# Attention values with v stationary: softmax weights stream, row sums from added weights, x turned back by a matmul

## The chip, the cores and the metric

The kernel runs on one core of a Trainium2 chip. The metric is device time in microseconds (us) from the first to the last instruction. The core has five engines with queues of their own: TensorE (PE in the profile; PEld is its weight load), VectorE (DVE), ScalarE (ACT), GpSimd (POOL) and SyncE (SP, which here only issues transfers). A TensorE matmul `mm(out, lhsT, rhs)` holds `lhsT` stationary and streams `rhs` through: the columns of `lhsT` become the partitions of the output, and `rhs` is what moves. All data are f32, and each f32 matmul appears as two records in the trace.

## The reference, cut to what matters

Attention over 8 batches, 8 heads, 576 positions and a head size of 64, with a bias from cumulated sums; then a mixture of 8 experts in which each token goes to one expert, either its own best (by the logits) or that of the token before it.

```python
scores = q @ k.T / sqrt(64)                        # causal, plus bias -(cum[i] - cum[j])
attn = exp(scores - max) / (sum + 1e-9)
x = (attn @ v) as (B, S, H*D)                      # D = 512 per token
logits = x @ w_gate;  local = sigmoid(x @ w_local)
for b, s in order:                                 # the expert is carried along the sequence
    e = argmax(logits[b, s]) if s == 0 or local < 0.5 else expert of s - 1
    out[b, s] = softmax(logits)[e] * (relu(x @ w1[e]) @ w2[e])
```

## The kernel before

Two heads make a pair, and there are 32 pairs (4 of each batch). Scores are computed turned: keys on partitions, queries along the columns, so that `sc` (the exponentials, called weights below) has keys on partitions. For one pair they come in four units of two PSUM banks each. `scores(n, u)` multiplies both heads (64 rows of the array each), ScalarE takes the exponentials, GpSimd zeroes the half above the diagonal. The last 64 keys against the last 64 queries are a tile of their own, `sct`.

```python
UNITS = (((1, 0, P, 2 * P), (0, 0, 0, 2 * P)),          # (key chunk, group, first query, end)
         ((0, 1, 2 * P, S), (3, 1, 3 * P, S)),
         ((1, 1, 2 * P, S),), ((2, 1, 2 * P, S),))
VW = DH + E + 2                                         # 64 of v, 9 value logits, a one: 74

def values(n, t):                                       # t: a tile of 128 queries; the fifth has 64
    if t < NF:
        for h in range(2):
            for c in range(t + 1):
                mm(po[:, t % 2, h, :], lhsT=weights(n, c, t, h), rhs=va[:, c, 2 * hp + h, :], ...)   # L369
        if t % 2:
            nc.vector.reciprocal(rec, po[:, :, :, VW - 1])
            for to, a, z in (("x", 0, DH), ("l", DH, VW - 1)):
                nc.vector.tensor_tensor(xs[b, to][...], po[:, :, :, a:z], rec..., op=Alu.mult)      # L375
    else:
        for c in range(NF):
            for h in range(2):
                mm(po[h * TL : h * TL + TL, :], lhsT=weights(n, c, NF, h), rhs=va[:, c, 2 * hp + h, :], ...)  # L381
        for h in range(2):
            mm(po[d, :], lhsT=scs[n, "t"][d, :], rhs=vl[d, hp, :], ...)                             # L385
        # ... cut: reciprocal and two products
```

Here the weights are stationary (128 columns) and v moves (74 columns). So that no product with `w_gate` is needed later, v carries its own logits: `value_logits` multiplies v (turned, `vT`, its own load) by `w_gate` and `w_local` (L284) and turns the result back into `va` (L296), once per batch. The one in the last column gives the sum of the weights. `logits` adds up the heads, and for the 64-row tile `logits_tail` folds two halves by a matmul (L407, `ltp`).

```python
for n in range(NPAIR + 1):                              # one attention step
    # ... cut: loads of the next batch
    scores(n, 0); scores(n, 1)
    values(n - 1, 0..2)
    # ... logits_tail once per batch; plan: sorting stages, scatters, weight loads
    scores(n, 2); scores(n, 3)
    values(n - 1, 3..4)
    # ... value_logits (hp >= 2), store and logits at a batch's end; plan
```

The tokens are sorted by expert while attention still runs: groups of batches (0, 1) and (2, 3, 4) pass through stages (choose, rows, hold, rank, gates) and scatter their rows of x to a buffer in memory; batches 5 to 7 are sorted in hooks of the expert stage. Four experts' first blocks of 128 tokens ("early" blocks) are fetched before attention ends.

```python
for bs, n0 in (((0, 1), 9), ((2, 3, 4), 21)):           # ... stages and two scatters per half step
at(28, 1, sort.early)
at(20, 0, lambda bank: load_weights(nc, ready["w"][0], w1, w2, 0))
last = sort.group((5, 6, 7), xs)
experts(..., [("early", e) for e in range(4)] + [("further", i) for i in range(SURE)], hooks, ...)

# experts: a block of 128 tokens
turn_x(i):   four transposes of x into PSUM, copied to xT            # L1023, L1025
layer1(i):   64 records hp <- w (stationary), xT (128 columns)       # L1040
layer2(i):   16 records yp <- hT (stationary), w (512 columns)       # L1052
load(i + 2): 4.2 MB of one expert's weights in 8 transfers           # L960
```

Of the kernel before, what the change touches and what calls it, by code (L numbers as in the profile page):

```python
# [32 lines left out]
XW = D + 2  # L33
R = N + P
EARLY = 4
SURE = NBLK - 2 - EARLY
MASKED = -1e9
VW = DH + E + 2
WR = 16
# [3 lines left out]

UNITS = (
    ((1, 0, P, 2 * P), (0, 0, 0, 2 * P)),
# [3 lines left out]
)  # L49


@with_exitstack
def kernel(
# [6 lines left out]
    vT: bass.AP,  # L60
# [19 lines left out]
    recs = const.tile([P, NPAIR, 2 * NF + 1], F32, name="recs")  # L80
# [3 lines left out]
    with ExitStack() as main:  # L84
# [4 lines left out]
        def new_x(b):  # L89
            xs[b] = keep.tile([P, NF, XW], F32, name="xb"), keep.tile([TL, XW], F32, name="xt")  # L90
            return xs[b]
# [7 lines left out]
        for bs, n0 in (((0, 1), 9), ((2, 3, 4), 21)):  # L99
            g = sort.group(bs, xs)  # L100
            for f, i in zip(g.stages, (1, 2, 3, 4, 4)):
                at(n0 + i // 2, i % 2, f)
            for i, f in enumerate(g.scatters):
                i = 5 + i // 2
                at(n0 + i // 2, i % 2, f)
        at(3, 1, sort.constants)
        at(28, 1, sort.early)
        gx = main.enter_context(tc.tile_pool(name="gx", bufs=5))
        ready = {"w": {0: wf.tile([P, DK * F + FK * D], F32, name="w")}, "x": {}}
        at(20, 0, lambda bank: load_weights(nc, ready["w"][0], w1, w2, 0))  # L110

        def fetch_early(bank):
            for e in range(EARLY):
                ready["x"][e] = gx.tile([P, XW], F32, name="xg")
                nc.sync.dma_start(ready["x"][e], rows_d[e * R : e * R + P, :])

        at(30, 0, fetch_early)
        last = sort.group((5, 6, 7), xs)

        tail = attention(tc, q, k, vm, vt, vT, s, w_gate, w_local, ident, lg, recs, const, new_x, plan)  # L120
# [5 lines left out]
                [("early", e) for e in range(EARLY)] + [("further", i) for i in range(SURE)], hooks, wf, gx, ready)  # L126
# [6 lines left out]
    wrong = nc.values_load(out_of[0:1, 0:1], min_val=0, max_val=P * NPAIR * (2 * NF + 1),  # L133
                           skip_runtime_bounds_check_because="a count of elements")
    with tc.If(wrong > 0):
        attention_general(tc, q, k, vm, vt, s, w_gate, w_local, cum_d, x_d, ident, lg)
        with ExitStack() as again:
# [8 lines left out]
            for bs in (range(0, 4), range(4, 8)):  # L146
                xs = {b: (pool.tile([P, NF, XW], F32, name=f"xb{b % 4}"), pool.tile([TL, XW], F32, name=f"xt{b % 4}"))
                      for b in bs}
                for b in bs:
                    r0 = b * S  # L150
                    nc.sync.dma_start(xs[b][0][:, :, :D], x_d[r0 : r0 + TS, :].rearrange("(t p) d -> p t d", p=P))
                    nc.sync.dma_start(xs[b][1][:, :D], x_d[r0 + TS : r0 + S, :])
                g = sort.group(bs, xs)
                for f in (*g.stages, *g.scatters):
                    f(bank)
# [6 lines left out]
def attention(ctx, tc, q, k, vm, vt, vT, s, w_gate, w_local, ident, lg, recs, keep, new_x, plan):  # L162
# [20 lines left out]
    p_vT = pool("p_vT", 1)  # L183
# [3 lines left out]
    ps_s = pool("ps_s", 3, space=PSUM)  # L187
    ps_o = pool("ps_o", 2, space=PSUM)

    ins, vTs, scs, vws, xs = {}, {}, {}, {}, {}  # L190

    first, rest, whole = slice(0, 1), slice(1, HP), slice(0, HP)

    def new_batch(b):
        qk = p_in.tile([P, 2, HP, S], F32, name="qk")
        ins[b] = [qk[:, i] for i in range(2)]
        vTs[b] = p_vT.tile([P, HP, S], F32, name="vTb")
# [5 lines left out]
    def load_vT(b, p):  # L203
        nc.sync.dma_start(vTs[b][:, p], vT[b][:, p])

    def load_v(b, p, eng=nc.sync):
        h = slice(2 * p.start, 2 * p.stop)
        for c in (slice(0, NF),) if p == whole else (slice(c, c + 1) for c in range(NF)):
            eng.dma_start(vas[b % 2][:, c, h, :DH], vm[b][:, c, h])

    def load_vl(b, eng=nc.sync):
        eng.dma_start(vls[b % 2][:, :, :DH], vt[b])
# [5 lines left out]
    vas = [(once if i else p_va).tile([P, NF, H, VW], F32, name=f"va{i}") for i in range(2)]  # L218
    vls = [once.tile([P, HP, VW], F32, name=f"vl{i}") for i in range(2)]
# [7 lines left out]
    load_v(0, first, nc.scalar)  # L227
    load_vT(0, first)
    load_vl(0, nc.scalar)
    load_qk(0, slice(1, 2), nc.scalar)  # L230
    load_vT(0, rest)
    load_v(0, rest)
    for i in range(2, HP):
        load_qk(0, slice(i, i + 1))
    wbd = once.tile([P, HP, 2 * WR], F32, name="wbd")
    nc.gpsimd.memset(wbd, 0.0)
    for h in range(2):
        for w, a, z in ((w_gate, 0, E), (w_local, E, E + 1)):
            nc.gpsimd.dma_start(wbd[h * DH : h * DH + DH, :, h * WR + a : h * WR + z],
                                w.rearrange("(a h d) e -> h d a e", h=2, d=DH)[h])  # L240
    for t in (*vas, *vls):
        nc.gpsimd.memset(t[..., VW - 1 : VW], 1.0)

    idle = ps_s.tile([P, 2, 512], F32, name="idle", tag="s")
    for i in range(10):
        mm(idle[:, 0, :P], lhsT=ident, rhs=ident, start=True, stop=True)
    fold = keep.tile([P, TL], F32, name="fold")
    nc.vector.tensor_tensor(fold, ident[:, :TL], ident[:, TL:], op=Alu.add)
# [3 lines left out]

# [4 lines left out]
    for g, (q0, q1) in enumerate(GROUPS):  # L257
        rel = t_in.tile([BH, q1], F32, name=f"rel{g}")
        nc.vector.tensor_scalar(rel, cum[:, :q1], cum[:, MIDS[g] : MIDS[g] + 1], None, Alu.subtract)
        for c in range(min(NF, q1 // P)):  # L260
            tr(bps[:, at : at + BH], rel[:, c * P : (c + 1) * P], ident[:BH, :BH])
            bias_of[g, c] = at
            at += BH
    for h in range(2):
        mm(bps[h * TL : h * TL + TL, at : at + NPAIR], lhsT=rel[:, TS:],
           rhs=ident[:BH, :BH].rearrange("k (n h) -> k h n", h=2)[:, h], start=True, stop=True)
    bias_of["tail"] = at
    bias = once.tile([P, at + NPAIR], F32, name="bias")
    nc.vector.tensor_copy(bias, bps[:, : at + NPAIR])
    tmp.close()  # L270
    p_sc = pool("p_sc", 2, reuse_waits="tile")
    p_sm = pool("p_sm", 2)

    def value_logits(b, step, p=whole):

        if b >= B:
            return
        va, vl = vas[b % 2], vls[b % 2]
        rows = slice(32 * p.start, 32 * p.stop)
        if step == 0:  # L280
            ps = ps_s.tile([P, 2, 512], F32, name="vwp", tag="s").rearrange("p a c -> p (a c)")
            for a, z in ((0, 512), (512, S)):
                for hp in range(p.start, p.stop):
                    mm(ps[hp * 32 : hp * 32 + 32, a:z], lhsT=wbd[:, hp, :], rhs=vTs[b][:, hp, a:z],  # L284
                       start=True, stop=True)
            if p.start == 0:
                vws[b] = p_sm.tile([P, NB * P], F32, name="vw")
            for i in range(p.start, p.stop) if p.start else (0,):
                r = slice(32 * i, 32 * i + 32) if p.start else rows
                nc.vector.tensor_copy(vws[b][r, :S], ps[r, :S])  # L290
                nc.vector.tensor_copy(vws[b][r, S:], ps[r, TS:S])
            return
        pt = ps_s.tile([P, 2, 512], F32, name="vwt", tag="s").rearrange("p a c -> p (a c)")
        n = rows.stop
        for c in range(NB):
            tr(pt[:, c * P : c * P + n], vws[b][:n, c * P : (c + 1) * P], ident[:n, :n])  # L296
        keyed = pt[:, : NB * P].rearrange("p (c h e) -> p c h e", c=NB, e=WR)
        hs = slice(2 * p.start, 2 * p.stop)
        nc.vector.tensor_copy(va[:, :, hs, DH : DH + E + 1], keyed[:, :NF, hs, : E + 1])
        for h in range(2):  # L300
            d = slice(h * TL, h * TL + TL)
            nc.vector.tensor_copy(vl[d, p, DH : DH + E + 1],
                                  keyed[d, NF, :, : E + 1].rearrange("p (a h) e -> p a h e", h=2)[:, p, h])

    def scores(n, u):
# [3 lines left out]
        heads = [slice(DH * h, DH * h + DH) for h in range(2)]  # L309
        tail = u == 0  # L310
        ps = ps_s.tile([P, 2, 512], F32, name="ps", tag="s")
        w = sum(q1 - q0 for _, _, q0, q1 in UNITS[u])
        sc = scs[n, u] = p_sc.tile([P, 2, w], F32, name=f"sc{u}")
        at, places = 0, []
        for c, g, q0, q1 in UNITS[u]:
            for h, d in enumerate(heads):
                mm(ps[:, h, at : at + q1 - q0], lhsT=kb[d, hp, c * P : c * P + P], rhs=qb[d, hp, q0:q1],  # L317
                   start=True, stop=True)
            places.append((c, g, q0, at, at + q1 - q0))
            at += q1 - q0  # L320
        if tail:
            for d in heads:
                mm(ps[d, 0, at : at + TL], lhsT=kb[d, hp, TS:], rhs=qb[d, hp, TS:], start=True, stop=True)  # L323
        diag = []
        for c, g, q0, a, z in places:
            for h in range(2):
                i = bias_of[g, c] + 2 * n + h
                nc.scalar.activation(sc[:, h, a:z], ps[:, h, a:z], Act.Exp, bias=bias[:, i : i + 1], scale=scale)  # L328
# [786 lines left out]
```

## Time and profile before

Median of three runs: 962.62 us (961.43 to 965.38). The profiled execution spans 964.8 us.

| stage | from, to (us) | what runs |
|---|---|---|
| start | 0 to 8.5 | loads, bias from the cumulated sums |
| attention | 8.5 to 344 | 33 steps |
| experts | 344 to 965 | 41 blocks of 128 tokens |

How to read the lines in the following part. A group's line gives the source line, the engine, the operation, output<-inputs, the shapes (for a matmul: stationary rows*columns, then output) and how often it ran. A timeline line gives the start, the length, the instruction group merged over neighbours, and how many. "PE x <- y" in the list of waits is what TensorE waited for: total us, times, the longest. "issue" is a wait for nothing that the profile shows. "PEclk" is the share of full clock that TensorE was granted. Matmuls are pipelined, so the time between two starts says more than the length of one.

### The profile page before, as it was taken

The numbers are of one execution on the slowest core, as the hardware profiler recorded it, in microseconds if no ns is written. First come the engines' busy times: TensorE is split into PE (matmuls) and PEld (weight loads), VectorE is DVE, ScalarE is ACT, GpSimd is POOL, SyncE is SP. The second block draws the span as 40 slices with busy tenths as digits, with TensorE's granted clock in tenths as the row PEclk, the third lists the DMA queues.
The fourth block names the chain that finished last, engine by engine and source line by source line (L and its number), as shares of the span: only waits on it lengthen the run. The fifth ranks groups of instructions, "written<-read, shape, count | busy, mean of one in ns | idle before, by whom it ended". The sixth has DMA issues, their size and how long they took to land.

```text
span 964.8 us, 16728 instructions
## 1 busy us (share of the span) xinstructions
PE 927.7 (96%) x6538; PEld 698.9 (72%) x6538; DVE 209.8 (22%) x649; ACT 182.0 (19%) x465; POOL 171.9 (18%) x329
## 2 busy tenths in 40 slices
PE   8999998999979996999999999999999999999995
PEld 5787786877758884677777777777777777677672
DVE  3222432224313243121111111111111111111110
ACT  3454544444525400000000000000000000000000
POOL 2221143121352206011011011011011011011000
PEclk8999998999979998999999999999999999999998
DMA  9463262637541658988988988988988988988950
GB/s 272 130 213 148 55 222 80 203 151 226 186 138 44 232 202 293 314 305 326 351 303 323 352 296 324 344 309 317 340 320 324 344 311 317 344 308 322 352 209 20
DMA packets 78332, 245.30 MB, mean 254 GB/s; under 512 B 21245, under 2 KB 21277, under 8 KB 75552
## 3 DMA queue, kind: packets, MB, share of 16 engines
q1 hardware_dynamic: 66480, 214.30, 63.7%
q0 software_dynamic: 9312, 28.68, 8.0%
q10 hardware_dynamic: 2448, 1.11, 0.5%
q8 instruction: 56, 0.92, 0.4%
q14 instruction: 36, 0.29, 0.1%
HBM read 220.67 MB, written 23.64 MB: 253 GB/s over the span
## 4 chain that ended last, share of the span: by engine, by line
PE 79%; DMA 2%; issue 2%; POOL 1%; DVE 1%; POOLq 0%; DVEq 0%
PE hp L1040 31%; PE yp L1052 29%; PE po L369 8%; PE ps L317 5%; DMA x_rows<-xb,r_slot_i 2%; PE xp L1023 2%; PE pot L381 1%; PE pot L385 0%; PE vwp L284 0%; PE ps L323 0%; POOL x_rows L947 0%; PE bank L876 0%; POOL sc L334 0%; PE vwt L296 0%; PE ltp L407 0%
## 5 line engine op out<-in xcount | busy, mean ns | idle before, releaser
L1040 PEld LDWEIGHTS hp<-xT,w 128*128 128x128 f32 x2624 | 301.1, 192 | 30.9 <-issue 29.1
L1040 PE MATMUL hp<-xT,w 128*128 128x128 f32 x2624 | 304.1, 276 | 10.2 <-issue 8.7
L1052 PE MATMUL yp<-w,hT 128*128 128x512 f32 x656 | 295.5, 594 | 0.0
L1052 PEld LDWEIGHTS yp<-w,hT 128*128 128x128 f32 x656 | 119.0, 191 | 119.6 <-issue 119.4
L328 ACT ACTIVATE sc<-ps,bias 128x320 f32<-128x320 f32 (+3 forms) x384 | 151.3, 486 | 168.3 <-PE ps L323 88.1
L369 PEld LDWEIGHTS po<-va,sc 128*128 128x128 f32 x1280 | 149.8, 194 | 25.5 <-issue 20.9
L369 PE MATMUL po<-va,sc 128*128 128x74 f32 x1280 | 159.3, 280 | 3.8 <-POOL sc L334 3.8
L1045 ACT ACTIVATE hT<-hp 128x512 f32<-128x512 f32 x41 | 24.5, 597 | 560.3 <-PE hp L1040 532.2
L1058 POOL DMA_INDIRECT out_dram<-y,at x41 | 40.9, 997 | 497.0 <-DVE y L1057 483.9
L317 PE MATMUL ps<-qk 64*128 64x320 f32 (+3 forms) x768 | 113.9, 417 | 0.0
L1043 DVE TENSOR_SCALAR hT<-hp 128x512 f32<-128x512 f32 x41 | 28.3, 691 | 261.0 <-PE hp L1040 261.0
L334 POOL TENSOR_SCALAR_AFFINE_SELECT sc<-sc 128x256 f32<-128x256 f32 (+1 forms) x96 | 47.6, 496 | 198.7 <-ACT sc L328 197.1
L317 PEld LDWEIGHTS ps<-qk 64*128 64x128 f32 x768 | 63.2, 193 | 18.2 <-issue 2.9
L1057 DVE TENSOR_SCALAR y<-yp,xg 128x512 f32<-128x512 f32 x41 | 30.8, 750 | 114.5 <-PE yp L1052 114.3
L1025 DVE COPY xT<-xp 128x512 f32<-128x512 f32 x41 | 28.3, 691 | 119.7 <-PE xp L1023 119.6
L373 DVE RECIPROCAL recs<-po 128x4 f32<-128x4 f32 x64 | 11.7, 183 | 185.9 <-PE po L369 183.5
L1023 PEld LDWEIGHTS xp<-ident,xg 128*128 128x128 f32 x164 | 20.4, 141 | 20.6 <-issue 20.6
L947 POOL DMA_INDIRECT x_rows<-xb,r_slot_i x32 | 31.4, 981 | 8.4 <-issue 7.3
L375 DVE TENSOR_TENSOR xb<-po,recs 128x256 f32<-128x256 f32 x64 | 27.2, 425 | 11.0 <-DMA x_rows<-xb,r_slot_i 8.6
L1023 PE MATMUL xp<-ident,xg 128*128 128x128 f32 x164 | 24.7, 273 | 0.0
L1016 POOL DMA_DIRECT2D xg<-x_rows x37 | 22.1, 598 | 12.2 <-DMA w<-in_w_dram 9.8
L381 PE MATMUL pot<-va,sc 128*64 128x74 f32 x512 | 23.5, 234 | 0.0
(140 smaller groups left out, 255.4 us busy)
## 6 DMA issues: line engine op xcount, KB each, us to landing
w<-in_w_dram SPq DMA_DIRECT2D x328, 512.0 KB
xg<-x_rows POOLq DMA_DIRECT2D x37, 257.0 KB
qk<-in_q_dram SPq DMA_DIRECT2D x7, 1152.0 KB
qk<-in_k_dram SPq DMA_DIRECT2D x7, 1152.0 KB
vTb<-in_vT_dram SPq DMA_DIRECT2D x7, 1152.0 KB
va<-in_vm_dram SPq DMA_DIRECT2D x7, 1024.0 KB
x_rows<-r_empty SPq DMA_DIRECT2D x13, 257.0 KB
qk<-in_q_dram SPq DMA_DIRECT2D x4, 288.0 KB
```

Source lines behind the costliest of these rows:

```text
L317: mm(ps[:, h, at : at + q1 - q0], lhsT=kb[d, hp, c * P : c * P + P], rhs=qb[d, hp, q0:q1], start=True, stop=True)
L328: nc.scalar.activation(sc[:, h, a:z], ps[:, h, a:z], Act.Exp, bias=bias[:, i : i + 1], scale=scale)
L334: nc.gpsimd.affine_select(out=x, in_=x, compare_op=Alu.is_ge, fill=0.0, base=0, pattern=[[0, 2], [0, len(diag)], [1, P]], channel_multipli ...
L369: mm(po[:, t % 2, h, :], lhsT=weights(n, c, t, h), rhs=va[:, c, 2 * hp + h, :], start=(c == 0), stop=(c == t))
L381: mm(po[h * TL : h * TL + TL, :], lhsT=weights(n, c, NF, h), rhs=va[:, c, 2 * hp + h, :], start=(c == 0), stop=False)
L947: self.s.nc.gpsimd.indirect_dma_start(out=next(self.s.views)[:, :], out_offset=bass.IndirectOffsetOnAxis(ap=self.slot[:z, m : m + 1], axis=0),
L1023: tr(ps[:, c, :], xg[i][:, c * P : (c + 1) * P], ident)
L1025: nc.vector.tensor_copy(xT[i], ps)
L1040: mm(ps[:, j, :], lhsT=w[:, c, f], rhs=xT[i][:, c, :], start=(c == 0), stop=(c == DK - 1))
L1052: mm(ps, lhsT=h[:, c, :], rhs=w[:, c, :], start=(c == 0), stop=(c == FK - 1))
L1057: nc.vector.tensor_scalar_mul(y, ps, xg[i][:, D + 1 : D + 2])
L1058: nc.gpsimd.indirect_dma_start(out=outs[i][:, :], out_offset=bass.IndirectOffsetOnAxis(ap=at[i][:, 0:1], axis=0), in_=y[:, :], element_off ...
```

## The change

v becomes stationary and the weights move. A group of queries (0 to 255, or 256 to 575) is one PSUM bank with the two heads on partitions 0 to 63 and 64 to 127, so x comes out turned: head size on partitions, queries along columns. The tail tile is gone; instead the last 128 keys (`KEYS[NF] = S - P`, those already counted masked out by a bias of -1e9) meet the last 64 queries. v's logits, `vT` and their matmuls are gone too. The sums of the weights come from VectorE adding the chunks of keys, and then matmuls with a column of ones. x, still turned and not divided, is turned back by a matmul against `turn`, which holds an identity with `w_gate` and `w_local` beside it, so that x and its logits come out together; the product with the reciprocal follows. x's row has 8 pieces of 73 (64 and 9), 586 words with identity and gate, in place of 514.

```diff
-VW = DH + E + 2
+HW = DH + E + 1
+X0 = E + 1
+XI = H * HW
+XW = XI + 2
-EARLY = 4
+EARLY = (0, 0, 1, 1)
 UNITS = (
-    ((1, 0, P, 2 * P), (0, 0, 0, 2 * P)),
+    ((1, 0, P, 2 * P), (0, 0, 0, 2 * P), (NF, 1, TS, S)),
...
-        for bs, n0 in (((0, 1), 9), ((2, 3, 4), 21)):
+        for bs in ((0, 1), (2, 3), (4,), (5,)):
+            n0 = HP * bs[-1] + HP + 1
             g = sort.group(bs, xs)
-            for f, i in zip(g.stages, (1, 2, 3, 4, 4)):
+            for f, i in zip(g.stages, (1, 3, 5, 7, 8)):
...
-        at(20, 0, lambda bank: load_weights(nc, ready["w"][0], w1, w2, 0))
+        for i in range(8):
+            at(16 + i // 2, i % 2, lambda bank, i=i: load_weights(nc, w, w1, w2, EARLY[0], (i,)))
-        last = sort.group((5, 6, 7), xs)
+        last = sort.group((6, 7), xs)
...
-    ps_s = pool("ps_s", 3, space=PSUM)
-    ps_o = pool("ps_o", 2, space=PSUM)
+    ps_s = pool("ps_s", 2, space=PSUM)
+    ps_o = pool("ps_o", 1, space=PSUM)        # four tags: o0, o1, b0, b1
...
-    for i in range(10):
-        mm(idle[:, 0, :P], lhsT=ident, rhs=ident, start=True, stop=True)
+    spin(18)                                  # warm-up matmuls; 8 more twice in the first step
...
+    def add_up(n):
+        add = nc.vector.tensor_tensor
+        add(low, piece(n, 0, 0, P), piece(n, 1, 0), op=Alu.add)
+        add(high, piece(n, 0, 1), piece(n, 1, 1), op=Alu.add)
+        for c in (2, 3, NF):
+            add(x, x, piece(n, c, 1), op=Alu.add)
+
+    def values(n, g, cs):
+        for c in cs:
+            for h in range(2):
+                mm(o[DH * h : DH * h + DH, a - q0 : z - q0], lhsT=vas[b % 2][:, c, 2 * hp + h, :], rhs=w[:, h],
+                   start=(c == 0), stop=(c == (1, NF)[g]))
+
+    def copy(n, g):
+        nc.vector.tensor_copy(x, xs["o", g][:, : q1 - q0])
+
+    def sums(n):                              # 20 matmuls of one column
+        for g in range(2):
+            for h in range(2):
+                for t, a, p in halves(g):     # 64 queries each
+                    mm(xs["o", 1][p : p + TL, i : i + 1], lhsT=w, rhs=one, start=True, stop=True)
+        nc.vector.reciprocal(recs[:, n], xs["o", 1][:, at : at + 2 * NB])
+
+    def rows(n, g, ps):                       # turning back: 4 or 5 halves, 146 columns each
+        for t, a, p in halves(g):
+            mm(ps[p : p + TL, t * 2 * HW : (t + 1) * 2 * HW], lhsT=xs["t", g][:, a : a + TL], rhs=w, ...)
+
+    def divide(n, g, ps):
+            nc.vector.tensor_tensor(x, y, rec.unsqueeze(3).to_broadcast([m, k, 2, HW]), op=Alu.mult)
...
         if n < NPAIR:
             scores(n, 0)
             scores(n, 1)
         if n:
-            for t in range(3):
-                values(n - 1, t)
+            values(n - 1, 0, (0, 1))
+            values(n - 1, 1, (0, 1))
+            add_up(n - 1)
+            copy(n - 1, 0)
+        if n > 1:
+            back(n - 2, 1)                    # rows and divide; logits at a batch's end
...
             scores(n, 2)
             scores(n, 3)
         if n:
-            for t in (3, 4):
-                values(n - 1, t)
+            values(n - 1, 1, (2, 3, NF))
+            sums(n - 1)
+            copy(n - 1, 1)
+            back(n - 1, 0)
```

The second part of the change is in the experts. The four early blocks are two of expert 0 and two of expert 1, and two neighbouring blocks of one expert share one set of weights; batch 5 is sorted inside attention too, in a group of its own, and batches 6 and 7 remain for the hooks.

```diff
+    for i, x in enumerate(blocks):
+        if not i or x[0] == "further" or x != blocks[i - 1]:
+            sets.append(x)
+        of.append(len(sets) - 1)
...
-        load(i + 2)
+        if i or not ready:
+            load(of[i] + 2)
```

The aim is to pay for fewer loads of stationary columns and to let both heads' values run at the same time, to free TensorE of the value logits, and to have fewer weights to fetch when the experts begin.

## The prediction

> **What bounds the kernel now.** I read the page first (busy shares), then the stretches table, then TensorE's timeline of one attention step, then the list of TensorE's waits. Shares and stretches (columns of the second fence: stretch and its length; busy us and instruction count of PE, PEld, DVE, ACT, POOL; granted clock; DMA share; GB/s):
>
> ```profile
> PE 927.7 (96%) x6538; PEld 698.9 (72%) x6538; DVE 209.8 (22%) x649; ACT 182.0 (19%) x465; POOL 171.9 (18%) x329
> ```
>
> ```profile
> 20.00:100.00 80.00, 80.00 (x780) 64.30 (x771) 24.25 (x97) 39.36 (x109) 18.82 (x56) 1.00 0.52 171
> 100.00:160.00 60.00, 57.45 (x530) 45.86 (x530) 20.61 (x88) 27.06 (x73) 21.02 (x44) 0.94 0.46 140
> 260.00:280.00 20.00, 12.02 (x98) 9.39 (x98) 2.90 (x13) 4.90 (x13) 10.62 (x16) 0.74 0.59 150
> 340.00:396.00 56.00, 45.78 (x294) 34.84 (x294) 20.21 (x70) 2.67 (x5) 16.77 (x23) 0.91 0.80 269
> 396.00:940.00 544.00, 544.00 (x3180) 399.62 (x3179) 83.93 (x154) 22.69 (x38) 59.13 (x75) 1.00 0.88 320
> ```
>
> TensorE is the bound: in 20 to 100 us and from 396 us on it is never idle at full clock. It is not full in three stretches: around 153 us, in 260 to 280 us, and at the seam between attention and experts (340 to 396 us). One attention step of the loop (pair n-1's values between pair n's scores), and the waits:
>
> ```profile
> 96.16 0.93 PE L317 MATMUL ps<-qk 64*128 64x128 f32 x8
> 97.01 0.33 PE L323 MATMUL ps<-qk 64*64 64x64 f32 x4
> 97.27 1.13 PE L317 MATMUL ps<-qk 64*128 64x320 f32 x8
> 98.34 2.90 PE L369 MATMUL po<-va,sc 128*128 128x74 f32 x24
> 101.17 0.28 PE L407 MATMUL ltp<-lt,fold 128*64 128x9 f32 x2
> 101.38 1.35 PE L317 MATMUL ps<-qk 64*128 64x320 f32 x8
> 102.66 2.01 PE L369 MATMUL po<-va,sc 128*128 128x74 f32 x16
> 104.59 0.73 PE L381 MATMUL pot<-va,sc 128*64 128x74 f32 x16
> 105.26 0.34 PE L385 MATMUL pot<-vl,sct 64*64 64x74 f32 x4
> 105.53 0.38 PE L317 MATMUL ps<-qk 64*128 64x128 f32 x2
> ```
>
> ```profile
> PE hp L1040 <- issue: 8.7, 9, 1.7
> PE ltp L407 <- DVE lb L375: 6.7, 1, 6.7
> PE po L369 <- POOL sc L334: 3.8, 2, 2.5
> ```
>
> Start to start the step is 9.37 us, without a gap. Of it L369 is 40 records in 2.83 + 1.93 = 4.76 us. An f32 matmul shows as two records.
>
> **What the Trainium skill says.** (1) "TensorE: Matmul & The Clock Gate", LDWEIGHTS: a load takes the stationary columns over 1.2 ns, whatever the rows: 107 ns for 128. The trace agrees: L369 moves only 74 columns, yet a record takes 1.93/16 = 0.12 us, so it is the load of 128 columns that is paid for. (2) Same page, Part 3 (packing small matmuls): outputs on different partitions use different column groups and run at the same time. The trace agrees: the 16 records of L381 (64 stationary columns, two heads on two halves) take 0.67 us, where 16 x 74 columns one after another would take 0.99 at the rate below. (3) "TensorEngine Tiling (Array Packing)": key properties: changing the tiling mode drains the engine; and under performance considerations it names exactly this swap of stationary and streaming operand. The remainders below are that drain. (4) The clock-gate page, Part 1: an idle window of about 3.4 us halves the clock. The trace agrees: the waits at 153 us and 273 us lie in the stretches with clocks 0.94 and 0.74.
>
> **The rates I use.** L1052 moves 512 columns in 3.60/8 = 0.45 us a record (0.43 between starts), so 0.84 ns a column and record, 1.68 ns a column of an f32 matmul; for two heads on two halves of the array, 1.68 ns a column of the pair. Check: the scores at 101.38 are two pairs of 320 columns, 640 x 1.68 = 1.08, measured 1.28: 0.20 remainder per run of row-tiled scores. L381: 4 pairs of 74, 0.50, measured 0.67: 0.17 per run of column-tiled matmuls.
>
> **The change part by part, one attention step on TensorE.**
> - Scores u0 and u1 lose the 64x64 tail (L323 and its two mode changes) and gain one pair of 64 columns: (128+256+64+320+192) = 960 x 1.68 + 0.20 = 1.81 us, where 98.34 - 96.16 = 2.18 are paid now. Scores u2, u3 stay at 1.28.
> - Values, first part: 256+128+320+320 = 1024 columns, 1.72 us. In the same tiling mode the turning back of the group of pair n-2: five halves of 146 columns, two pairs and one alone, 3 x 146 x 1.68 = 0.74. With 0.17: 2.63 us.
> - Values, second part: 320+192+64 = 576 columns, 0.97 us. Sums: 20 matmuls of one moving column, 40 records, 20 pairs of records; bound by loading 64 columns, half of the 0.116 us that 128 take: 20 x 0.058 = 1.16. Turning back the first group: 2 x 146 x 1.68 = 0.49. With 0.17: 2.79 us.
> - Sum: 1.81 + 2.63 + 1.28 + 2.79 = 8.51 us. Against it stand 9.37 less 0.21 of ltp (101.17 to 101.38) = 9.16 us of the plain step, plus, once per four steps, ltp 0.21, the transposes of the value logits 0.69 and their product 1.11 (86.30 to 86.99 and 76.02 to 77.13 in the timeline), which all go: 9.16 + 2.01/4 = 9.66. **Gain 1.15 us a step, over 32 steps 37 us.**
> - VectorE gains the additions. From rows of the trace (128x256 425 ns, 128x301 470, 128x344 520: about 1.07 ns an element and 0.15 us each) the five of 256, 640, 640, 384 and 128 elements take 2.9 us; two copies of 256 and 320 columns 0.9, three products 1.25, the reciprocal 0.2: about 5.2 us a step in place of 2. It lies beside TensorE, and the order leaves room: the additions are done 3.5 us into the step and the sums come at about 7.
> - ScalarE: two exps of 128x320, 128x256 and so on stay; one of 64 columns on both heads becomes two of 331 ns. By their means 2 x 363 + 2 x 478 + 6 x 537 + 2 x 466 + 2 x 331 = 6.5 us: below 8.51.
> - The stalls. The 6.7 us behind lb (L375) is a tile of x that batch 2's scatters still read when batch 6 wants it. With groups (0,1), (2,3), (4), (5) those scatters go out at steps 21 to 23, batch 6 first writes at 25: gone. With its clock loss and the 3.8 us behind GpSimd's selects and theirs, some 15 us are lost now (10.5 idle, about 3.4 at half clock after 153 us, 1.7 after 273 us). I keep 3 for the scatters, two in every half step as before, so 12 come free.
> - Added: four groups sorted inside attention in place of two, about 1.5 us of small matmuls and mode changes each, +3; and the score buffers fall from three to two, so a sorting stage that holds one makes the next scores wait for VectorE, some 0.7 us in two stages of four groups, +5.
> - Expert stage: 41 blocks before and 41 after: with the counts of experts 0 and 1 after five batches (435 and 301) both early blocks of each are full. From 396 us on nothing in a block changes; the rows grow from 514 to 586 words, 0.04 MB on each fetch and 4.2 MB of weights: hidden. At the seam about 13 us are lost now: 8.7 in waits that the profile gives no releaser for, the rest clock and first copies. Four early blocks then need two sets of weights, not four, and 10 scatters stand there in place of 15. I can't name the cause of the 8.7, so I count on half of the 13, and take 3 off for the longer chain of VectorE before the last sort (product, logits, choice): -3.
>
> Sum: 962.6 - 37 - 12 + 3 + 5 - 3 = 918.6. The start gives perhaps 2 back (18 warm-up matmuls and 8 more twice keep the clock up, and hold the bias transposes back a little): **917 us.**
>
> **The rivals.**
> - The sums don't overlap. If a load of 64 columns and its matmul took 0.06 us each record, unpaired, the sums would cost 2.4 us: +1.2 a step, +40 us, 955 us. For it: nothing in the trace has one moving column; L407's two records cost 0.21 us. Against it: that is nearly all mode change, and L381's pairs do overlap.
> - The long moving operands of two column groups don't run together: values 2.7 us more a step, over 1000 us. Against it: L381 does it with 74 columns, and the scores do it by rows with 320.
> - The two score buffers or VectorE become the wait: by mean durations ScalarE has emptied u1 at about 5.0 us of a step, and u3 asks for it at 5.1. In the trace eight exps of 320 follow one another at 0.41 us, not 0.54, which leaves more. If it bites at 0.3 us a step, +10 us.
> - The stalls stay: scatters and selects still share GpSimd, and each stall over 3 us costs clock too: +10 us.
> - The seam clears altogether: -8 us.
>
> **Range and chances.** The step's arithmetic is good to 0.4 us a step (13 us), stalls and seam to 10 us together: 899 to 939. Slower than 981 needs the second rival; within 2% (943 to 982) needs the first one or two smaller ones together. Faster 0.91, same 0.07, slower 0.02.
>
> **What would show it.** Steps of 8.4 to 8.6 us between the first scores in 20 to 100 us; the values at 1.68 ns a column of a pair; the 40 records of the sums in 1.1 to 1.3 us; the attention stage ending near 300 us in place of 342; no wait of several us before 300; still about 14.7 us a block afterwards ((964.8 - 396.8) us over some 38.6 blocks). It would be wrong if the sums' line shows over 2 us a step, if scores wait for ScalarE in each step, or if TensorE waits for the added weights.

## The result and the profile after

| | before | changed | ratio, with its 95% interval |
|---|---|---|---|
| chip A (the runs of the prediction) | 963.24 us (961.43 to 965.38) | 908.16 us (907.76 to 908.47) | 0.9427 [0.9406, 0.9448] |
| chip C (the same two kernels again) | 969.89 us (965.62 to 974.97) | 918.67 us (916.88 to 921.67) | 0.9480 [0.9448, 0.9512] |

The change takes off 55 us in the first place and 51 in the other; 46 were predicted. The record does not name the chip of the first runs, called A here. Where not said otherwise, lines of the changed kernel are of the execution on chip A, which spans 906.7 us (964.8 before).

First the busy shares, then the stretches table of the changed kernel, with the columns as in the table of before:

```profile
PE 889.4 (98%) x7239; PEld 652.0 (72%) x7239; DVE 307.6 (34%) x741; ACT 187.5 (21%) x496; POOL 191.1 (21%) x292
```

```profile
20.00:100.00 80.00, 80.00 (x1066) 58.12 (x1065) 49.00 (x116) 47.05 (x131) 24.20 (x51) 1.00 0.34 117
100.00:160.00 60.00, 58.95 (x772) 43.03 (x772) 41.71 (x101) 33.05 (x94) 27.19 (x41) 1.00 0.52 176
260.00:280.00 20.00, 20.00 (x258) 14.65 (x254) 13.83 (x41) 12.14 (x35) 7.94 (x12) 1.00 0.21 79
340.00:396.00 56.00, 56.00 (x328) 41.04 (x327) 9.44 (x19) 2.39 (x4) 6.61 (x10) 1.00 0.81 309
```

TensorE is still the bound, and now almost without holes (58.95 of 60 us in the second stretch, all of the others): the clocks of 0.94, 0.74 and 0.91 are 1.00. VectorE has gone from 24 to 49 us in the first 80, beside TensorE. TensorE's timeline of one attention step:

```profile
275.61 2.01 PE L290 MATMUL ps<-qk 64*128 64x128 f32 x20
277.55 1.95 PE L338 MATMUL o<-sc,va 128*64 128x256 f32 x16
279.33 0.91 PE L369 MATMUL b<-turn,xT 128*64 128x146 f32 x10
280.17 1.35 PE L290 MATMUL ps<-qk 64*128 64x320 f32 x8
281.44 1.20 PE L338 MATMUL o<-sc,va 128*64 128x320 f32 x12
282.47 0.23 PE L362 MATMUL o<-one,sc 128*64 128x1 f32 x4
...
282.80 0.96 PE L362 MATMUL o<-one,sum 128*64 128x1 f32 x28
283.61 0.70 PE L369 MATMUL b<-turn,xT 128*64 128x146 f32 x8
```

The next scores start at 284.24, so the step is 8.63 us: scores 1.94, values 1.78, turning back 0.84, scores 1.27, values 1.03, sums 1.14, turning back 0.63. TensorE's waits are all short (us in total, times, longest):

```profile
PE ps L290 <- DVE r_v L862: 2.8, 4, 0.7
...
PE ps L290 <- DVE r_rank L898: 0.4, 1, 0.4
```

The 6.7 us behind `lb`, the 3.8 behind GpSimd's selects and the 8.7 of "issue" at the seam are gone. The first matmul of the experts, `hp`, starts at 299.4 us where it started at 344.4 before: attention gives 45.0 us. From there to the end it is 607.3 us in place of 620.4: the seam gives 13.1. A later block takes 14.45 us in both kernels, and nearly all of the 13.1 is the third block: from its first `hp` to that of the fourth are 27.3 us before and 14.45 here.

### The profile page after: what moved, and what is told of

It is laid out like the page before. It is cut to its first block, busy times and chain, and to the rows that moved or that the text cites. A ratio compares the mean times of both kernels' runs of the same rounds, so it can differ in the third digit from the quotient of the medians.

```text
span 906.7 us, 18152 instructions
## 1 busy us (share of the span) xinstructions
PE 889.4 (98%) x7239; PEld 652.0 (72%) x7239; DVE 307.6 (34%) x741; ACT 187.5 (21%) x496; POOL 191.1 (21%) x292
## 4 chain that ended last, share of the span: by engine, by line
PE 98%; DVE 1%; issue 0%; POOL 0%; POOLq 0%; DVEq 0%
PE hp L1024 32%; PE yp L1036 31%; PE ps L290 11%; PE o L338 11%; PE b L369 4%; PE o L362 4%; PE xp L1007 2%; PE idle L254 1%; DVE r_u L861 0%; DVE r_v L862 0%; PE bank L857 0%; PE bank L872 0%; PE bank L890 0%; PE bank L891 0%; POOL out_dram L1042 0%
## 5 line engine op out<-in xcount | busy, mean ns | idle before, releaser
L296 ACT ACTIVATE sc<-ps,bias 128x320 f32<-128x320 f32 (+4 forms) x448 | 160.7, 467 | 116.8 <-issue 56.4
L290 PE MATMUL ps<-qk 64*128 64x320 f32 (+4 forms) x896 | 109.1, 377 | 3.1 <-DVE r_v L862 2.8
L338 PE MATMUL o<-sc,va 128*64 128x320 f32 (+4 forms) x896 | 100.8, 364 | 0.0
L338 PEld LDWEIGHTS o<-sc,va 128*64 128x64 f32 x896 | 56.8, 136 | 42.3 <-issue 18.6
L325 DVE TENSOR_TENSOR sum<-sum,sc 128x640 f32<-128x640 f32 (+2 forms) x96 | 61.5, 641 | 10.1 <-POOL sc L302 5.2
L369 PE MATMUL b<-turn,xT 128*64 128x146 f32 x566 | 50.5, 291 | 0.0
L369 PEld LDWEIGHTS b<-turn,xT 128*64 128x64 f32 x566 | 38.6, 137 | 7.8
L362 PE MATMUL o<-one,sum 128*64 128x1 f32 x1024 | 38.3, 197 | 0.0
L382 DVE TENSOR_TENSOR xb<-b,recs 128x292 f32<-128x292 f32 (+1 forms) x94 | 35.4, 404 | 7.7 <-PE b L369 7.6
L362 PEld LDWEIGHTS o<-one,sum 128*64 128x64 f32 x1024 | 35.5, 138 | 0.0
```

Of the source, the lines that this page charges most:

```text
L290: mm(ps[:, h, at : at + z - a], lhsT=kb[d, hp, KEYS[c] : KEYS[c] + P], rhs=qb[d, hp, a:z], start=True, stop=True)
L296: nc.scalar.activation(sc[:, h, at : at + z - a], ps[:, h, at : at + z - a], Act.Exp, bias=bias[:, i : i + 1], scale=scale)
L325: add(x, x, piece(n, c, 1), op=Alu.add)
L338: mm(o[DH * h : DH * h + DH, a - q0 : z - q0], lhsT=vas[b % 2][:, c, 2 * hp + h, :], rhs=w[:, h], start=(c == 0), stop=(c == (1, NF)[g]))
L362: mm(xs["o", 1][p : p + TL, i : i + 1], lhsT=w, rhs=one, start=True, stop=True)
L369: mm(ps[p : p + TL, t * 2 * HW : (t + 1) * 2 * HW], lhsT=xs["t", g][:, a : a + TL], rhs=w, start=True, stop=True)
```

## The experiments

My theory: the gain is TensorE's shorter step (fewer stationary columns loaded, both heads at once), plus stalls that the new sorting groups take away. The rivals: moving columns are what was paid for; the column groups or the sums hardly overlap; VectorE is about to become the bound; and, for the 13 us at the seam, that it is the early blocks in twos, or the shorter last sorting group, or nothing in the change at all. The runs come from three places: A above, which may be one of the other two chips at another time; chip B (before: 968.61 us); chip C (before: 971.64 us beside the first four kernels there, 969.89 beside the last four). Kernels are compared on one chip, or through their ratio to before.

### What the groups and the twos bring alone (chip B)

**b1_twos**: before, with the early blocks in twos of an expert.

```diff
-EARLY = 4
+EARLY = (0, 0, 1, 1)
...                                        # cut: two blocks of an expert share one set of weights
-        load(i + 2)
+        if i or not ready:
+            load(of[i] + 2)
```

> The kernel before with only the early blocks in twos of an expert. Theory W: the seam clears: 950 to 953 us in place of 963. Theory S: 961 to 965 us.

970.85 us (965.28 to 978.42), ratio 1.001 [0.9985, 1.0035]. The twos alone bring nothing, and the issue waits at the seam stayed (10.0 us). The third block takes 29.2 us (27.3 in before). So fewer weights in flight there are not what clears it.

**b2_groups**: before, with the sorting groups and stages of the change.

```diff
-        for bs, n0 in (((0, 1), 9), ((2, 3, 4), 21)):
+        for bs in ((0, 1), (2, 3), (4,), (5,)):
+            n0 = HP * bs[-1] + HP + 1
-            for f, i in zip(g.stages, (1, 2, 3, 4, 4)):
+            for f, i in zip(g.stages, (1, 3, 5, 7, 8)):
...                                        # cut: scatters and early blocks at other steps
-        last = sort.group((5, 6, 7), xs)
+        last = sort.group((6, 7), xs)
```

> The kernel before with only the groups, stages and scatters of the changed one (batches (0,1), (2,3), (4), (5) inside attention, (6,7) left; early blocks still of four experts). The 6.7 us wait for a tile of x, whose scatters then come four steps sooner, should go with its clock loss, about 8 us; the GpSimd waits of 3.8 us may stay. Theory W for the seam: 953 to 957 us (attention alone). Theory S: seam too: 941 to 947 us.

949.71 us (948.96 to 949.81), ratio 0.9792 [0.9749, 0.9835]: the groups alone take off 16 to 24 us. Its stretches show where:

```profile
100.00:160.00 60.00, 60.00 (x586) 47.63 (x585) 22.24 (x94) 27.91 (x76) 18.87 (x41) 1.00 0.43 132
260.00:280.00 20.00, 20.00 (x201) 15.50 (x199) 9.39 (x41) 9.44 (x27) 8.82 (x17) 1.00 0.46 120
340.00:396.00 56.00, 52.14 (x297) 38.57 (x295) 17.33 (x53) 2.37 (x4) 13.34 (x18) 0.94 0.92 310
```

Both stalls of attention are gone, with their clock loss; the seam (last line) still stalls, but less: 3.9 us of "issue" where b1 has 10.0, and a third block of 22.0 us where b1 has 29.2. By the trace's clock records TensorE spent 34 us at half clock in before (44 in b1), and 10 here, the idle end of each execution left out. By difference, some 30 us of the change are left for the turned-round values; no run has them alone.

### What a step pays for (chip C)

**b3_wide_v**: before, with 106 moving columns in place of 74 in the values, 32 of them unused.

```diff
-                    mm(po[:, t % 2, h, :], lhsT=weights(n, c, t, h), rhs=va[:, c, 2 * hp + h, :],
+                    j = (2 * hp + h) * VW - 32 * h
+                    mm(po[:, t % 2, h, :], lhsT=weights(n, c, t, h),
+                       rhs=va[:, c].rearrange("p h w -> p (h w)")[:, j : j + VW + 32],
```

> The kernel before with 106 moving columns in place of 74 in the values matmuls of the four tiles of 128 queries (32 neighbouring columns of v more, not read afterwards; three more small VectorE operations a pair of tiles). Theory: these matmuls pay for loading 128 stationary columns, and a record of 106 columns (0.089 us) still hides under a load of 0.116 us: 962 to 966 us. Rival: the columns that move are what is paid for: 20 x 32 x 1.68 ns = 1.07 us a step, 34 us, 997 us.

966.28 us (963.8 to 969.5), ratio 0.9956 [0.9935, 0.9978]. The timeline's two runs of values:

```profile
97.75 2.93 PE L370 MATMUL po<-va,sc 128*128 128x106 f32 x24
...
102.09 2.03 PE L370 MATMUL po<-va,sc 128*128 128x106 f32 x16
```

They start 2.86 and 1.97 us before what follows them (100.61 and 104.06), 2.83 and 1.93 before: 43% more columns cost 0.07 us in 4.76. The loads of 128 stationary columns were paid for, as the first step of the prediction had it.

**e3_heads_apart**: changed, with all of one head's values ahead of the other's.

```diff
-        for c in cs:
-            for h in range(2):
+        for h in range(2):
+            for c in cs:
```

> The changed kernel with the loops of the values matmuls turned round: all key chunks of one head, then all of the other, in place of the two heads in turn. The same matmuls and columns. Theory: the two column groups run together only when neighbours in the queue lie on different groups; then the values' 1600 columns a step cost 1.68 ns twice, +2.7 us less what the ends of the runs still overlap, 2 to 2.7 us a step, 64 to 86 us: 970 to 995 us. Rival: the engine finds the overlap itself: 907 to 910 us.

942.44 us (941.74 to 942.84), ratio 0.9710 [0.9673, 0.9747]: 24 us above the changed kernel, between the two theories. The second part of the values, by the timeline:

```profile
84.75 1.51 PE L338 MATMUL o<-sc,va 128*64 128x320 f32 x9
85.94 0.28 PE L362 MATMUL o<-one,sc 128*64 128x1 f32 x2
86.10 0.38 PE L338 MATMUL o<-sc,va 128*64 128x192 f32 x2
```

Sums of one head (L362) start between values of the other (L338): each half of the array goes through its own matmuls. The step is 9.22 us (78.91 to 88.13), 0.59 more. The first part, where two matmuls of a head stand in a row, lasts 1.77 us as before (80.86 to 82.63); only the second, with three in a row, got longer. So the halves do run at once with long moving operands, even where the program doesn't interleave them well. 32 x 0.59 = 19 us is the step; the rest goes with more time at half clock (13.7 us against 3.4 in the changed kernel there), half of it after one wait of 3.8 us for a score buffer.

**e4_sums_twice**: changed, with each matmul of the sums issued twice.

```diff
-                    for p in (p, P - TL) if 2 * g + t == NF else (p,):
+                    for p in (p, P - TL, p, P - TL) if 2 * g + t == NF else (p, p):
```

> The changed kernel with each of the 20 sum matmuls of a step issued twice in a row (the result is the same). If sums cost what loading 64 columns in two groups costs, they add 1.1 us a step, 36 us: 942 to 946 us; but the doubles lie on one column group in turn, so if the groups don't overlap for neighbours on the same half, up to 2.3 us a step, 980 us. If moving one column were hidden altogether: 908 us.

986.51 us (983.41 to 988.4), ratio 1.0156 [1.0111, 1.0201]: 68 us above the changed kernel. The timeline of TensorE, and two stretches of it:

```profile
22.09 1.83 PE L362 MATMUL o<-one,sum 128*64 128x1 f32 x56
...
24.40 3.06 PE L290 MATMUL ps<-qk 64*128 64x128 f32 x20
27.38 2.53 PE L338 MATMUL o<-sc,va 128*64 128x256 f32 x16
```

```profile
25.50:28.50 3.00, 3.00 (x16) 1.81 (x16) 2.52 (x4) 2.71 (x9) 1.15 (x2) 0.50 0.02 7
29.00:33.00 4.00, 4.00 (x43) 2.53 (x39) 0.98 (x3) 1.62 (x5) 0.42 (x1) 1.00 0.00 0
```

The sums take 2.31 us (85.33 to 87.64 in a step at full clock) in place of 1.14: the second twenty cost 1.17, as much as the first, 58 ns a matmul with its two records, both halves at once. That is 37 of the 68 us. The rest was in nobody's theory: right behind the sums the clock falls to 0.50, though TensorE is busy in every one of these microseconds (3.00 of 3.00), and in the 3.4 us before as well. Scores that take 1.94 us take 2.98 (27.38 - 24.40). In all it spent 64.9 us at half clock, 61.5 more than the changed kernel there: 31 us. 37 + 31 = 68.

**e5_adds_twice**: changed, with VectorE's five additions of a step done twice.

```diff
+        idle = p_sm.tile([P, 2, S - 2 * P], F32, name="idle1")
+        low = p_sm.tile([P, 2, P], F32, name="idle0")
+        add(low, piece(n, 0, 0, P), piece(n, 1, 0), op=Alu.add)
+        add(idle, piece(n, 0, 1), piece(n, 1, 1), op=Alu.add)
...                                        # cut: the other three
```

> The changed kernel with VectorE's five additions made a second time into a tile that nobody reads: 2.9 us a step more of VectorE, 8.1 of 8.6 us then. Theory: VectorE lies beside TensorE: 908 to 912 us. Rival: the step follows VectorE (products, copies and reciprocals come later, or GpSimd's selects are slowed): over 925 us.

956.07 us (955.47 to 957.69), ratio 0.9857 [0.9819, 0.9895]: 37 us above the changed kernel. Stretches, and the longest of TensorE's waits:

```profile
20.00:100.00 80.00, 80.00 (x1076) 58.22 (x1076) 72.53 (x158) 46.80 (x131) 27.28 (x50) 1.00 0.36 120
100.00:160.00 60.00, 53.36 (x626) 38.54 (x626) 51.81 (x118) 26.57 (x74) 25.67 (x34) 0.91 0.37 126
```

```profile
PE b L376 <- DVE xT L351: 19.8, 13, 3.5
```

Until sorting starts, VectorE at 7.8 us of the 8.63 us step (72.53 in 80) costs nothing. Once the sorting stages come on top, from about 100 us on, the copy `xT` comes late 13 times, and 51 us in all pass at half clock. So VectorE is not the bound of the changed kernel, but its room is 3.3 us a step, and the sorting needs a part of it.

### The seam (chips B, then C)

**e1_four_experts** is the changed kernel with early blocks of four experts, **e2_three_left** with three batches left for the last group.

```diff
-EARLY = (0, 0, 1, 1)
+EARLY = (0, 1, 2, 3)                                  # e1
-        if i or not ready:
-            load(of[i] + 2)
+        load(of[i] + 2)                               # e1
...
-        for bs in ((0, 1), (2, 3), (4,), (5,)):
-        last = sort.group((6, 7), xs)
+        for bs in ((0, 1), (2, 3), (4,)):             # e2
+        last = sort.group((5, 6, 7), xs)
```

> The changed kernel with its four early blocks of four experts again (all else as changed). The trace of the kernel before loses some 13 us at the seam of attention and experts, the changed one about 1. Theory W (weights): two sets of weights in place of four for the first four blocks is what cleared the seam; then this run loses it again: 917 to 922 us, and TensorE waits within the third block. Theory S (scatters): it was the smaller last group, 10 scatters in place of 15; then this run stays at 907 to 910 us.

> The changed kernel with batches 5, 6 and 7 sorted in the hooks of the expert stage, as before the change (early blocks in twos kept). Theory S: 15 scatters at the seam bring the waits back: 917 to 922 us. Theory W: 907 to 910 us. If attention gains something by one group less (a wait of 0.7 us and some matmuls): up to 2 us less in either case.

On chip B e1 took 921.82 us (920.14 to 926.84), ratio 0.9513 [0.9459, 0.9567], and e2 922.56 us (921.67 to 923.44), ratio 0.9513 [0.9471, 0.9556]. Both looked 8 us worse than 0.9427. But e1 had lost 8.4 us before `hp`, in steps whose instructions are those of the changed kernel (10.2 us there passed at half clock, which costs 5), and at the seam both stalled by "issue". Two unlike edits with one loss, part of it where nothing was edited, pointed at the chip. So both ran again on chip C, with the changed kernel beside them.

> The changed kernel a second time, beside the other three on one chip. If the seam between attention and experts is cleared by what the change does, the time is 908 us again, the first hp matmul comes at about 299 us and no run of hp matmuls 0.70 us apart shows. If the clear seam was chance of the one run, the seam shows such a run of about 10 us here too and the time is 915 to 920 us.

> The changed kernel with early blocks of four experts again, now beside the changed kernel on one chip. If early blocks in twos of an expert are what clears the seam (fewer weights moving there), this is slower by 8 to 14 us, with the slow run of hp matmuls at the seam here and not in the changed kernel. If the slow run comes and goes with the chip or the execution, the two are within 4 us of each other.

> The changed kernel with three batches left for the last sorting group again, beside the changed kernel. If the ten scatters in place of fifteen at the seam clear it, this is slower by 8 to 14 us, by the slow run at the seam. If the slow run comes and goes with the chip or the execution, it is slower by at most 5 us, for the longer last sort alone.

| chip C | us | ratio to before |
|---|---|---|
| after_again (the changed kernel) | 918.67 (916.88 to 921.67) | 0.9480 [0.9448, 0.9512] |
| e1b_four_experts | 920.25 (918.74 to 920.95) | 0.9486 [0.9447, 0.9526] |
| e2b_three_left | 921.59 (920.65 to 922.77) | 0.9502 [0.9463, 0.9541] |

They are 1.6 and 2.9 us from the changed kernel, and that one now stalls at the seam too, though for less than e2b. TensorE's waits there, after_again first, then e2b:

```profile
PE hp L1024 <- issue: 3.8, 4, 1.7
```

```profile
PE hp L1024 <- issue: 9.2, 9, 1.7
```

The place in the timeline of after_again (the bracket is the idle time before a piece):

```profile
334.03 0.27 PE L1024 MATMUL hp<-xT,w 128*128 128x128 f32 x1 [1.03 <-issue]
...
336.83 3.49 PE L1024 MATMUL hp<-xT,w 128*128 128x128 f32 x17 [1.72 <-issue]
```

The same stutter in before, on chip A:

```profile
379.93 0.38 PE L1040 MATMUL hp<-xT,w 128*128 128x128 f32 x1 [1.15 <-issue]
382.03 0.37 PE L1040 MATMUL hp<-xT,w 128*128 128x128 f32 x1 [1.72 <-issue]
```

Matmuls that follow one another at 0.11 us elsewhere come at multiples of about 0.70 us, and a stretch at half clock follows. Of the fourteen traces only that of the changed kernel on chip A has none of it. The length of the third block tells what the stall costs (14.45 us without it):

| batches left for the last group | scatters | traces | third block, us |
|---|---|---|---|
| three | 15 | before, b1, b3, e2, e2b | 26.2 to 29.2 |
| two | 10 | b2, e1, e1b, after_again, e3 to e6 | 20.7 to 22.0 |
| two | 10 | the changed kernel on chip A | 14.45 |

So the shorter last group does not clear the seam, but it halves the stall, on both chips. The medians hide part of this: in the profiled executions e2b needs 620.0 us from `hp` to the end and after_again 613.6, and e2b is ahead by 0.9 us before that. The twos change nothing that can be told from noise (e1b 21.3 us, after_again 20.7). What cleared the rest on chip A is nothing in the change, for the same program stalls on chip C.

The stall starts 10.3 to 11.1 us after the first scatter of the last group in all thirteen traces that have it, and in the nine of the changed kernel and its variants it ends 4.1 to 4.9 us after the last scatter starts. That ties it to the scatters by timing and number; the ten scatters on chip A (318.6 to 330.0 us) did no such thing, so they are not enough by themselves. How they would hold up TensorE stays open, and spreading them was not tried.

### A version that is faster (chip C)

**e6_better**: changed, with a sorting stage working in the PSUM banks of the turned-back rows, so that it no longer holds a score buffer; the odd half of the second group turned back for its two heads on two column groups; and fewer warm-up matmuls in the first step.

```diff
     def bank(n):
-        t = ps_s.tile([P, 2, 512], F32, name="bank", tag="s")
-        return [t[:, i] for i in range(n)]
+        return [ps_o.tile([P, 512], F32, name=f"b{g}", tag=f"b{g}") for g in (1, 0)[:n]]
     # rows
+            for h, p in ((slice(0, HW), 0), (slice(HW, 2 * HW), TL)) if g and t == 2 else ((slice(0, 2 * HW), p),):
...                                        # cut: VectorE divides that half in two products, one a head
     # first step
-            spin(8)
+            spin(4)                                  # and none in its second half
```

> The changed kernel with three small edits: a sorting stage takes the PSUM banks of the turned-back rows in place of a score buffer, the odd 64-query half of the second group is turned back for its two heads on two column groups at once (73 moving columns in place of 146), and the first step has 4 and 0 warm-up matmuls in place of 8 and 8. From the changed kernel's trace: the waits of the scores for r_v and r_rank (3.2 us together) go, 73 x 1.68 ns = 0.12 us a step over 32 steps is 4 us, and the start gives 2: 8 to 9 us below the changed kernel on the same chip, 899 to 901 us. If the sorting stages then wait for the turned-back rows in place of the scores, the first 3 us stay; if the two column groups don't overlap, the 4 us stay: 904 to 907 us.

910.24 us (908.65 to 910.41), ratio 0.9384 [0.9351, 0.9418], beside 918.67 for the changed kernel: 8.4 us less, with no `r_v` or `r_rank` among its waits. One line of its timeline answers to the one at 279.33 above:

```profile
281.67 0.79 PE L370 MATMUL b<-turn,xT 128*64 128x146 f32 x12
```

Twelve records, in two places 73 columns wide, end 0.72 us later (scores at 282.39) where ten took 0.84: the 0.12 us a step. The scores of the third step start 1.9 us sooner (21.67 for 23.56 in after_again). Each term held, while the absolute 899 to 901 us, reckoned from chip A, did not.

## Why the prediction was right

The total lies 9 us under 917 on chip A and 2 over it on chip C. The second is partly luck: before was 7 us slower there, and the gain was 51 us for the 46 predicted. By its own steps, chip A, from the profiled executions (964.8 - 906.7 = 58.1 us; that of before lay 3 us above its median):

- **The step, 8.51 us and 37 us in all.** It is 8.63, so 9.66 - 8.63 = 1.03 us a step and 33 us. Values and turning back came to 2.62 (2.63 predicted), the second scores to 1.27 (1.28), the last part to 2.80 (2.79). What was short is the first scores, 1.94 for 1.81: five pairs carry a remainder of 0.33 above 960 x 1.68 ns, not the 0.20 that two pairs show, so the remainder is not only the drain that the prediction took it for. By the starts of single records most of the rest lies at the added pair of 64 columns: its second record and the one behind it last 0.111 us (276.424 to 276.535) and 0.325 (to 276.860), where the columns alone give 0.054 and 0.269. The pair loads 128 stationary columns to move 64; that this load is what it pays for fits b3's 0.116 us a record, but was not tested. The prediction priced it by its moving columns, against its own first point.
- **The rates.** 128 stationary columns are what was paid for (b3), a column of a pair costs 1.68 ns also in the values, and the sums cost 1.14 us for 1.16. The rival of sums that don't overlap is refuted by e4's timeline, that of column groups by e3's first part.
- **VectorE 5.2, ScalarE 6.5 us a step, beside TensorE.** From the first stretch, 49.00/80 x 8.63 = 5.3 and 47.05/80 x 8.63 = 5.1; ScalarE's term was 1.4 too high, as the sum of mean lengths of exps that overlap. e5 shows how much room VectorE had.
- **Stalls, sorting and score buffers, net 4 us (12 - 3 - 5).** Of attention's 45.0 us, 33.0 are the step and 1.7 the start (second step at 15.55 in place of 17.21 us); 10.3 remain for this sum. The direction was right, and b2 shows the stalls go by the groups. The size was not. Summed over the steps, all that exceeds the regular step in the changed kernel is 10.5 us: 3.2 us of waits for score buffers (5 predicted) and 7.3 for sorting four groups, 1.8 a group (1.5 predicted), so 3.6 for the two more. The stalls then gave about 17 us by difference (10.3 + 3.2 + 3.6), where 12 were counted: the 3 us kept for the scatters were not needed, as no wait of TensorE in attention names them.
- **The seam, -3.** This term was mis-sized: -13.1 on chip A, which was the last rival. On chip C the experts take 613.6 us, 6.8 less than before on chip A. There the count of half of the 13 holds, and the traces show what goes with it: a last group of two batches in place of three, which takes the third block from 26.2 to 29.2 us to 20.7 to 22.0. That the prediction hit on a half without a cause was luck, and the fewer sets of weights, which it named first, show no part in it. The 3 us taken off for VectorE's longer chain did not come: the first two blocks take 25.0 us (25.1 before). The cause of the stall itself, and of its absence on chip A, stays open.
- **The start, -2.** It gave 1.7.

Two errors cancel in part: 4 us too much from the step, 6 too little from the stalls; another 10 are the seam on chip A. That makes 12 us too little, of which 3 belong to the profiled execution of before.

The clock deserves a paragraph of its own. The prediction used "TensorE: Matmul & The Clock Gate", Part 1, for the loss behind waits, and said that an idle window of about 3.4 us halves the clock. The same part explains the gate as a monitor of how busy TensorE has been over a window of about 3.4 us, but its table names only an idle window as what halves the clock. The traces differ. In before the wait at 153 us is 2.55 us long, and the clock had fallen to 0.50 at 151.45, 1.07 us into it. In e4 the clock halves with no idle time, after 2.3 us of matmuls that move one column. The changed kernel, with 1.14 us of them in a step, never fell within attention on chips A and C, but is near it: in e1, on chip B, the clock fell at 149.3 and 261.9 us with 0.4 and 0.6 us of idle time in the 3.4 before.

## What to carry to other kernels

Where a matmul moves fewer columns than it loads, turn it round, so that the wide operand moves and two heads share the array on two column groups; price it from the trace as loads, moving columns and mode changes, and check that the new work on the other engines fits beside it together with what is already there. Look for a stall's buffer before its engine: regrouping the sort was worth 16 to 24 of the 50 us, about 6 of them at the seam. And a loss for which the profile names no releaser should be measured again, on a second chip, before an edit gets the credit; the length of the stalled block in every trace then showed what the totals did not.

## What the hardware showed that I had not expected

- The clock falls without idle time: with 40 one-column matmuls in a row in each step TensorE spent 64.9 us at half clock (e4). The clock fell thirteen times within attention, and eleven times TensorE had not been idle in the 6.8 us before.
- The halves of the array run ahead of each other. In e3 the program puts three f32 matmuls of head 0 (320, 192, 64 columns: six records) before those of head 1, yet head 1's first record starts at 85.345 us, ahead of three of head 0's at 85.502, 85.664 and 85.720. "TensorE: Matmul & The Clock Gate", Part 3 (the mechanism), says matmuls start in program order; this trace shows otherwise for two column groups, if the compiled program keeps the order of the source, which the trace does not tell.
- GpSimd's selects slow down beside VectorE's additions. The larger shape by the groups of instructions, changed kernel first, before second:

```profile
L302 POOL TENSOR_SCALAR_AFFINE_SELECT sc<-sc 128x512 f32<-128x512 f32 x32 | 27.6, 864 | 86.6 <-ACT sc L296 59.8 <-DVE sum L325 24.7 <-issue 2.0
```

```profile
L334 POOL TENSOR_SCALAR_AFFINE_SELECT sc<-sc 128x512 f32<-128x512 f32 x32 | 20.5, 641 | 110.2 <-ACT sc L328 110.2
```

  Its mean (after the first bar: busy us, mean ns) goes from 641 to 864 ns. "GPSIMD Engine Reference", Specifications, says that GpSimd shares its SBUF interfaces with VectorE and contends with its instructions of two SBUF inputs, which the additions are; the means agree, and with the additions doubled (e5) that of the 128x256 selects goes on from 497 to 585 ns (423 in before). It cost nothing here, for no wait of TensorE names GpSimd.
